# Rows of x stored in step order, the first expert's first 256 rows fetched and turned in the last two attention steps, and its first layer done in two column ranges

## The chip, the cores and the metric

The kernel runs on one core of one Trainium2 chip. The metric is the device time of one execution in microseconds (us). All tensors are float32 in memory. The engines are TensorE (PE, with its weight loads as PEld), VectorE (DVE), ScalarE (ACT), GpSimd (POOL) and SyncE (SP); SP, ACT and POOL also issue transfers (DMA), each through a queue of its own, in the order of the program.

## What is computed

Two blocks, one after the other. The first is an mLSTM cell over 4 batches, 8 heads, 768 positions and head width 40. Per head it carries a matrix state C, a normalizer n and a running maximum m, and its output is gated:

```python
m_new = np.maximum(f_gate[:, :, t] + m, i_gate[:, :, t])
f_stab = np.exp(f_gate[:, :, t] + m - m_new)
i_stab = np.exp(i_gate[:, :, t] - m_new)
C = f_stab * C + i_stab * outer(v_t, k_t);  n = f_stab * n + i_stab * k_t
y_t = sigmoid(o_gate_t) * (C @ q_t) / max(|n @ q_t|, 1.0)
```

(The broadcasts are shortened here.) Its output becomes x, 3072 rows of 320 numbers, one row per token, in the order batch, position. The second block is a mixture of 8 experts: a token goes to the expert that a hash of its id names, and the expert is two layers:

```python
expert_idx = token_ids * np.int64(2654435761) % np.int64(E)
for e in range(E):
    mask = expert_idx == e
    h = np.maximum(x[mask] @ w1[e], 0.0)     # w1: 320 x 1024
    out[mask] = h @ w2[e]                    # w2: 1024 x 320
```

## The kernel before

**Attention.** The cell is done in chunks of 128 positions. There are 24 steps, `for s in range(NT)` (L689); step s handles batch `s % 4` and chunk `s // 4` (`place`, L163). The order of instructions on every engine is written out by hand: each engine runs its instructions in program order and waits on semaphores. A step s does, in this order: transfers for later steps and the stores that are due (`waiting`, L711), on SP; `divided(s-1)` on DVE (L419 to L427: numerator by denominator, giving x of the step before); turns of keys and queries for s+2 (L304); pieces of the routing, spread over the steps by a table (`pieces`, L618); `scores(s+1)` (L350); `decays(s+1)` (L312: two exponentials on ACT, and `qs` on DVE, L332); up to two `gated` on POOL (L429: x times the output gate, L431); `state(s)` (L378); `weigh(s+1)` on DVE (L359, two instructions at L362); `attend(s)` on PE (L399, matmuls at L408 and L414). A gated tile is stored to the DRAM tensor `x_rows` two steps later (L736, `store` L433), at its token's place: row `b * S + c * P`.

**Routing.** Each token gets a slot: `route_counts` (L500) counts by one matmul, one scan along the 24 tiles and one addition the rank of each token among those of its expert; an expert has 416 slots, 384 in three tiles of 128 and 32 in a remainder that four experts share. `route_index` (L609, in step 21) makes from the slots two tables of row numbers: `g_idx`, from which rows are gathered, and `s_idx`, to which they are scattered. Tokens enter as numbers `tokv` (L445), which before follow batch and position, so that both tables hold the same numbers.

**Experts.** After the 24 steps come the last stores (L768), then the experts. `fetch(e)` (L863) issues on POOL three indirect gathers of 128 rows (L777) and, for the first expert of a group of four, a fourth for the remainder (`xr`). `turns(e)` (L872) turns each tile by three PE transposes (L797, L799, with a DVE copy of the last 64 columns between, L798) and a copy out of PSUM by DVE or ACT (L801, L803); the remainder's piece ends in a small POOL copy into the 32 last columns of `xT` (L883). `layer1` (L805) takes eight blocks of hidden features, two at a time: per pair four whole matmuls (L821) and two half-height ones (L814), each of 416 columns and each shown as two instructions in the profile, and two relus (DVE L828, ACT L830). `layer2` (L846) multiplies back (L850), and the rows are scattered (L784). Between the blocks of expert e, the tiles of expert e+1 are turned (`one`, L910), and for expert 0 the weights of experts 1 and 2 are asked for on ACT's queue.

At the border the order is: `fetch(0)`, `fetch(1)`, all four turns of expert 0, `fetch(2)`, `layer1` of expert 0 (L897 to L921). So POOL has seven gathers ahead of the copy L883. The PSUM banks of the experts are those of the attention steps, and become free with their last readers.

Of the kernel before, what the change touches and what calls it, by code (L numbers as in the profile page):

```python
# [8 lines left out]
F32 = mybir.dt.float32  # L9
BF16 = mybir.dt.bfloat16  # L10
I32 = mybir.dt.int32
I64 = mybir.dt.int64
AX = mybir.AxisListType.X
AF = mybir.ActivationFunctionType
ALU = mybir.AluOpType
PSUM = bass.MemoryType.PSUM

P = 128
# [4 lines left out]
def kernel(  # L23
# [24 lines left out]
    nc = tc.nc  # L48
    B, H, S, D = q.shape
    BH = B * H  # L50
    NB = S // P
    N = B * S
    Dm = H * D
    E, _, F = moe_w1.shape
    FB = F // P
    NT = N // P
# [1 line left out]
    DP = 64  # L58
    D1 = D + 1
    assert NB * P == S and FB * P == F and D <= DP and H % 2 == 0 and BH <= 32 and NB % 2 == 0  # L60
    assert E & (E - 1) == 0 and 2654435761 % E == 1

    dch = [(d0, min(P, Dm - d0)) for d0 in range(0, Dm, P)]
    DB = len(dch)

    NJ = 3
# [3 lines left out]
    CAP = NM + RM  # L70
    NR = E * NJ
    NX = -(-(N - CAP) // P)
    NC = NR + E // EG + NX
# [3 lines left out]
    wpools = [ctx.enter_context(tc.tile_pool(name="wpool", bufs=1))]  # L77
    w2pools = [ctx.enter_context(tc.tile_pool(name="w2pool", bufs=1))]

    x_d = nc.dram_tensor("x_rows", (N, Dm), F32, kind="Internal").ap()  # L80

    ident = consts.tile([P, P], F32, name="ident")
    g_idx = consts.tile([P, NC], I32, name="g_idx")
# [3 lines left out]
    def weights(src1, src2, wpool, w2pool, eng=None):  # L87

        eng = eng or nc.sync
        w1t = wpool.tile([P, 2, F], F32, name="w1t")  # L90
        w1c = wpool.tile([P, FB // 2, P], F32, name="w1c")
        w2t = w2pool.tile([P, FB, Dm], F32, name="w2t")
        eng.dma_start(w1t[:], src1[: 2 * P, :].rearrange("(a p) f -> p a f", p=P))
        last = src1[2 * P :, :].rearrange("d (a two f) -> two d a f", two=2, f=P)
        for i in range(2):
            eng.dma_start(w1c[i * P // 2 : (i + 1) * P // 2], last[i])
        eng.dma_start(w2t[:], src2.rearrange("(a p) d -> p a d", p=P))
        return w1t, w1c, w2t

    W = {}  # L100

# [30 lines left out]
    with tc.tile_pool(name="gates", bufs=1) as gp, \  # L132
# [30 lines left out]
        def place(s):  # L163
            return s % B, s // B
# [182 lines left out]
        def sigmoid(g):  # L347
            nc.scalar.activation(og[g][:], og[g][:], AF.Sigmoid)
# [82 lines left out]
            nc.gpsimd.tensor_tensor(x[:], x[:], og[s // NG][:, s % NG], op=ALU.mult)  # L431

        def store(s):  # L433
            b, c = place(s)
            r = b * S + c * P
            nc.sync.dma_start(x_d[r : r + P, :], st.pop(s)["x"].rearrange("p h d -> p (h d)"))

        iotas = {}
        for name, shape, pattern, base, mult in (
            ("experts", [P, E], [[1, E]], 0, 0),  # L440
            ("b2off", [P, E], [[-RM, E]], E * RM - RM, 0),
            ("thr", [P, NX], [[P, NX]], CAP, 0),
            ("kx", [1, NX], [[1, NX]], 0, 0),
            ("iota_f", [P, P], [[1, P]], 0, 0),
            ("tokv", [P, NT], [[P, NB], [S, B]], 1, 1),  # L445
        ):
            iotas[name] = (
                gp.tile(shape, I32, name=name + "_i"), gp.tile(shape, F32, name=name), pattern, base, mult,
            )
# [50 lines left out]
        def route_counts():  # L500
            cps = ps.tile([P, 2, E, NT], F32, name="cps", tag="tr", bufs=2)
            for i, t in enumerate((lt_m1, ones_sq)):
                nc.tensor.matmul(cps[:, i], lhsT=t[:], rhs=sel[:], start=True, stop=True)
            nc.vector.tensor_tensor_scan(
                pr.rearrange("p e t -> p (e t)"), keep_t.rearrange("p e t -> p (e t)"),
                cps[:, 1].rearrange("p e t -> p (e t)"), 0.0, op0=ALU.mult, op1=ALU.add,
            )
            nc.vector.tensor_tensor(rk[:], pr[:], cps[:, 0], op=ALU.add)

# [99 lines left out]
        def route_index():  # L609

            ta = gp.tile([P, NC], F32, name="ta")
            nc.vector.tensor_scalar(ta[:], tv[:], scalar1=-1.0, scalar2=0.0, op0=ALU.add, op1=ALU.max)
            nc.vector.tensor_copy(g_idx[:], ta[:])
            nc.vector.tensor_scalar(ta[:], tv[:], scalar1=0.0, scalar2=float(2 * N), op0=ALU.is_equal, op1=ALU.mult)
            nc.vector.scalar_tensor_tensor(ta[:], in0=tv[:], scalar=-1.0, in1=ta[:], op0=ALU.add, op1=ALU.add)
            nc.vector.tensor_copy(s_idx[:], ta[:])

        pieces = {  # L618
# [12 lines left out]
        o_at = {}  # L631
        for i, j in enumerate((2, 2, 3, 3, 4, 4, 5, 5, 6, 7, 8, 8, 9, 10, 10, 11, 12, 13, 13, 14, 15, 15, 16, 16)):
            o_at.setdefault(j, []).append(i)

        def unread(n):
            t = ps.tile([P, P], F32, name="un", tag="xh", bufs=2)
# [52 lines left out]
        for s in range(NT):  # L689
# [43 lines left out]
            for i in range(2):  # L733
                if ndone < s and ndone // NG <= nsig and s - 1 not in sig_at:
                    gated(ndone)
                    waiting.setdefault(min(s + 2, NT), []).append(ndone)  # L736
                    ndone += 1
            state(s)
            if s + 1 < NT:
# [6 lines left out]
            if s in sig_at:  # L746
                nsig = sig_at[s]
                sigmoid(nsig)
            attend(s)
            if s == 2:  # L750
                g1.weights(kwT1)
            if s == 3:
# [20 lines left out]
    xp = ctx.enter_context(tc.tile_pool(name="xp", bufs=2))  # L773
    mps = ctx.enter_context(tc.tile_pool(name="mps", bufs=2, space=PSUM))

    def gather(xg, idx):
        nc.gpsimd.indirect_dma_start(  # L777
            out=xg, out_offset=None, in_=x_d[:, :], in_offset=bass.IndirectOffsetOnAxis(ap=idx, axis=0),
        )

    def scatter(zp, idx, apart):
        zo = xp.tile([P, Dm], F32, name="zo", bufs=4)
        nc.scalar.copy(zo[:], zp[:])  # L783
# [18 lines left out]
        else:  # L802
            nc.vector.tensor_copy(dst, tp[:])  # L803

    def layer1(w, xT, h, cols, between=lambda fp: None):  # L805

        w1t, w1c, _ = w
        for fp in range(FB // 2):
            hp = [mps.tile([P, CAP], F32, name="mh", bufs=4) for _ in range(2)]

            def halves(first):
                for i in range(2):
                    r = slice(i * P // 2, (i + 1) * P // 2)
                    nc.tensor.matmul(  # L814
                        hp[i][:, :cols], lhsT=w1c[r, fp, :], rhs=xT[r, 2, :cols], start=first, stop=not first,
                    )

            def whole(i, first):
                fb = 2 * fp + i
                for db in range(2):  # L820
                    nc.tensor.matmul(  # L821
                        hp[i][:, :cols], lhsT=w1t[:, db, fb * P : (fb + 1) * P], rhs=xT[:, db, :cols],
                        start=(first and db == 0), stop=(not first and db == 1),
                    )

            def out(i):
                if i == 0:
                    nc.vector.tensor_relu(h[:, 2 * fp, :cols], hp[i][:, :cols])  # L828
                else:
                    nc.scalar.activation(h[:, 2 * fp + 1, :cols], hp[i][:, :cols], AF.Relu)  # L830

            if fp % 2 == 0:
                for i in range(2):
                    whole(i, True)
                between(fp)
                halves(False)
                for i in range(2):
                    out(i)
            else:
                halves(True)  # L840
                for i in range(2):
                    whole(i, False)
                    out(i)
                between(fp)
# [15 lines left out]
    with tc.manual_schedule():  # L860
        xgs, xTs, remT, hrem = {}, {}, {}, {}

        def fetch(e):  # L863
            if e % EG == 0:
                xgs[-1 - e // EG] = xp.tile([P, DB * P], F32, name="xr")
            xgs[e] = xp.tile([P, NJ, DB * P], F32, name="xg", bufs=3)
            for j in range(NJ):
                gather(xgs[e][:, j, :Dm], cols_of(g_idx, e * NJ)(j))
            if e % EG == 0:
                gather(xgs[-1 - e // EG][:, :Dm], cols_of(g_idx, NR + e // EG)(0))  # L870

        def turns(e):  # L872
            xT = xTs[e] = xp.tile([P, DB, CAP], F32, name="xT")

            def tile_of(j):
                turn(xgs[e][:, j, :], xT[:, :, j * P : (j + 1) * P], j % 2 == 1)

            def remainder():
                i = e % EG
                if i == 0:  # L880
                    remT[e // EG] = xp.tile([P, DB, P], F32, name="remT")
                    turn(xgs[-1 - e // EG], remT[e // EG][:], True)
                nc.gpsimd.tensor_copy(xT[:, :, NM:], remT[e // EG][:, :, i * RM : (i + 1) * RM])  # L883

            return [lambda j=j: tile_of(j) for j in range(NJ)] + [remainder]
# [10 lines left out]

        fetch(0)  # L897
        fetch(1)
        for piece in turns(0):
            piece()  # L900
        for e in range(E):
            g, i = e // EG, e % EG
            if e + 2 < E:
                fetch(e + 2)
            h = xp.tile([P, FB, CAP], F32, name="h")
            if i == 0:
                hrem[g] = xp.tile([P, EG, FB, RM], F32, name="hrem")
            ahead = turns(e + 1) if e + 1 < E else []
# [9 lines left out]
                if j == 0 and i == EG - 1:  # L918
                    rest(g)

            layer1(W[e], xTs[e], h, CAP, one)  # L921
            nc.gpsimd.tensor_copy(hrem[g][:, i], h[:, :, NM:])  # L922
            layer2(W[e], h, NJ, cols_of(s_idx, e * NJ), True, after)
            if e + 3 < E:
# [3 lines left out]
    with tc.If(nx > 0):  # L928
        with tc.For_i(0, nx, 1) as k:
# [10 lines left out]
            h = xp.tile([P, FB, CAP], F32, name="h")  # L940
            gather(xr[:, :Dm], gs[:, 0:1])
            turn(xr, xT[:, :, :P], False)
            layer1(w, xT, h, P)
            layer2(w, h, 1, lambda j: gs[:, 1:2], False)


# [28 lines left out]
```

## Time and profile before

| | us |
|---|---|
| median of 3 runs | 400.91 (400.55 to 402.49) |
| the profiled execution | 402.59 |
| its span, first to last instruction | 400.8 |
| PE busy | 370.8 (93%) |
| POOL busy | 144.4 (36%) |
| DVE busy | 137.7 (34%) |
| ACT busy | 111.9 (28%) |
| clock granted to PE, mean over the span | 0.964 |

The page divides the span into 40 slices of 10.02 us; a digit is the busy share in tenths. The timeline lists instructions by start, length, engine, line, and output and inputs; "idle before" names how long the engine stood still and what ended it. The chain of waits follows the last instruction back to whatever released each step. Matmul ends are modelled, and neighbours overlap in the listing, so I take distances from start to start where a stream is dense.

### The profile page before, as it was taken

The numbers are of one execution on the slowest core, as the hardware profiler recorded it, in microseconds if no ns is written. First come the engines' busy times: TensorE is split into PE (matmuls) and PEld (weight loads), VectorE is DVE, ScalarE is ACT, GpSimd is POOL, SyncE is SP. The second block draws the span as 40 slices with busy tenths as digits, with TensorE's granted clock in tenths as the row PEclk, the third lists the DMA queues.
The fourth block names the chain that finished last, engine by engine and source line by source line (L and its number), as shares of the span: only waits on it lengthen the run. The fifth ranks groups of instructions, "written<-read, shape, count | busy, mean of one in ns | idle before, by whom it ended". The sixth has DMA issues, their size and how long they took to land.

```text
span 400.8 us, 7874 instructions
## 1 busy us (share of the span) xinstructions
PE 370.8 (93%) x3163; PEld 253.5 (63%) x3163; DVE 137.7 (34%) x345; ACT 111.9 (28%) x227; POOL 144.4 (36%) x247
## 2 busy tenths in 40 slices
PE   8699879999999728999999999999999999999992
PEld 8487668788888614565575575555575575574561
DVE  8657657797878711201202101101201101101100
ACT  5386475566485200110101101101110101101100
POOL 8342428897987254014025013025024011010020
PEclk9899998999999956999999999999999999999997
DMA  6688998989899338892082182252092000000000
GB/s 133 122 157 147 172 172 158 200 174 196 172 224 264 117 94 276 272 338 80 7 281 87 34 271 65 82 179 87 18 278 84 2 33 15 2 33 16 0 20 32
DMA packets 124220, 51.02 MB, mean 127 GB/s; under 512 B 104338, under 2 KB 120174, under 8 KB 124182
## 3 DMA queue, kind: packets, MB, share of 16 engines
q1 hardware_dynamic: 116614, 36.73, 39.4%
q0 software_dynamic: 2496, 8.20, 6.5%
q10 hardware_dynamic: 5072, 5.57, 4.6%
q8 instruction: 26, 0.43, 0.4%
q14 instruction: 12, 0.10, 0.1%
HBM read 42.10 MB, written 8.71 MB: 127 GB/s over the span
## 4 chain that ended last, share of the span: by engine, by line
PE 71%; issue 8%; POOL 8%; DMA 5%; DVE 3%; ACT 2%; SPq 2%; POOLq 0%; DVEq 0%; ACTq 0%
PE mh L821 23%; PE zp L850 23%; PE mh L814 6%; PE tr L309 4%; PE sp L356 4%; POOL x L431 3%; PE xh L414 2%; PE ab L320 2%; PE tp L797 1%; PE xh L408 1%; PE xh L387 1%; PE zp L891 1%; POOL C L397 1%; DMA x_rows<-x 1%; DMA xr<-x_rows,g_idx 1%
## 5 line engine op out<-in xcount | busy, mean ns | idle before, releaser
L850 PE MATMUL zp<-w2t,h 128*128 128x320 f32 x384 | 105.2, 433 | 0.0
L821 PE MATMUL mh<-xT,w1t 128*128 128x416 f32 x256 | 98.4, 529 | 0.9 <-issue 0.9
L850 PEld LDWEIGHTS zp<-w2t,h 128*128 128x128 f32 x384 | 72.7, 190 | 32.1 <-issue 3.3
L821 PEld LDWEIGHTS mh<-xT,w1t 128*128 128x128 f32 x256 | 47.7, 194 | 44.0 <-issue 42.9
L784 POOL DMA_INDIRECT out_dram<-zo,s_idx x26 | 25.7, 987 | 92.5 <-ACT zo L783 92.5
L803 DVE COPY xT<-tp 128x384 f32<-128x384 f32 x16 | 8.9, 558 | 142.5 <-PE tp L799 103.2
L830 ACT ACTIVATE h<-mh 128x416 f32<-128x416 f32 x32 | 16.6, 517 | 109.6 <-PE mh L814 59.8
L783 ACT COPY zo<-zp 128x320 f32<-128x320 f32 x26 | 11.1, 426 | 101.1 <-PE zp L850 92.9
L828 DVE TENSOR_SCALAR h<-mh 128x416 f32<-128x416 f32 x32 | 18.9, 592 | 53.4 <-PE mh L821 26.9
L414 PE MATMUL xh<-v,w 128*64 128x41 f32 x768 | 34.8, 222 | 0.3 <-DVE w L362 0.3
L362 DVE TENSOR_TENSOR w<-sp,w 128x512 f32<-128x512 f32 x48 | 30.8, 682 | 12.2 <-ACT w L324 12.2
L922 POOL COPY hrem<-h 128x256 f32<-128x256 f32 x8 | 3.2, 400 | 83.7 <-ACT h L830 83.7
L324 ACT ACTIVATE w<-ab 128x512 f32<-128x512 f32 x48 | 26.0, 594 | 18.9 <-PE ab L320 18.9
L414 PEld LDWEIGHTS xh<-v,w 128*64 128x64 f32 x768 | 30.7, 138 | 0.4 <-DVE w L362 0.4
L356 PE MATMUL sp<-qT,kT 64*128 64x128 f32 x384 | 30.0, 294 | 0.1
L356 PEld LDWEIGHTS sp<-qT,kT 64*128 64x128 f32 x384 | 25.0, 195 | 4.4 <-issue 2.8
L408 PE MATMUL xh<-C,qs 128*64 128x82 f32 x320 | 27.4, 250 | 0.0
L777 POOL DMA_INDIRECT xg<-x_rows,g_idx x24 | 23.5, 978 | 9.7 <-issue 9.7
L814 PE MATMUL mh<-xT,w1c 64*128 64x416 f32 x128 | 26.7, 535 | 0.0
L397 POOL TENSOR_TENSOR C<-C,add 64x164 f32<-64x164 f32 x32 | 17.7, 553 | 20.8 <-ACT add L391 19.6
L431 POOL TENSOR_TENSOR x<-x,og 128x320 f32<-128x320 f32 x24 | 20.5, 871 | 9.4 <-DVE x L427 9.4
L309 PE MATMUL tr<-ident,q 128*128 128x128 f32 x96 | 15.3, 283 | 4.6 <-ACT dec L334 2.5
(177 smaller groups left out, 390.6 us busy)
## 6 DMA issues: line engine op xcount, KB each, us to landing
w2t<-in_moe_w_dram SPq DMA_DIRECT2D x5, 1280.0 KB
w1t<-in_moe_w_dram SPq DMA_DIRECT2D x5, 1024.0 KB
k<-in_k_dram SPq DMA_DIRECT2D x24, 160.0 KB
v<-in_v_dram SPq DMA_DIRECT2D x24, 160.0 KB
og<-in_o_gate_dram SPq DMA_DIRECT2D x24, 160.0 KB
x_rows<-x SPq DMA_DIRECT2D x24, 160.0 KB
q<-in_q_dram SPq DMA_DIRECT2D x23, 160.0 KB
w2t<-in_moe_w_dram ACTq DMA_DIRECT2D x2, 1280.0 KB
```

The costliest lines, as they stand in the source:

```text
L309: nc.tensor.transpose(tp[:, j, :], d[what][:, 2 * j : 2 * j + 2, :].rearrange("p h d -> p (h d)"), ident[:])
L324: nc.scalar.activation(w[:, hf], ab[:], AF.Exp)
L356: nc.tensor.matmul(sp[hf][:, j, :], lhsT=d["kT"][r, j, :], rhs=d["qT"][r, j, :], start=True, stop=True)
L362: nc.vector.tensor_tensor(d["w"][:, hf], d["sp"][hf][:], d["w"][:, hf], op=ALU.mult)
L408: nc.tensor.matmul(xh[t, 2 * j : 2 * j + 2, :], lhsT=d["qs"][:, j, t], rhs=Cs[b][c % 2][:, j].rearrange("p h d -> p (h d)"), start=True, s ...
L414: nc.tensor.matmul(hs[t, 2 * j + hf, :], lhsT=d["w"][:, hf, j, t], rhs=d["v"][:, 2 * j + hf, :], start=(c == 0), stop=True, skip_group_che ...
L431: nc.gpsimd.tensor_tensor(x[:], x[:], og[s // NG][:, s % NG], op=ALU.mult)
L777: nc.gpsimd.indirect_dma_start(out=xg, out_offset=None, in_=x_d[:, :], in_offset=bass.IndirectOffsetOnAxis(ap=idx, axis=0),)
L784: ins = nc.gpsimd.indirect_dma_start(out=out[:, :], out_offset=bass.IndirectOffsetOnAxis(ap=idx, axis=0), in_=zo[:], in_offset=None, bound ...
L814: nc.tensor.matmul(hp[i][:, :cols], lhsT=w1c[r, fp, :], rhs=xT[r, 2, :cols], start=first, stop=not first,)
L821: nc.tensor.matmul(hp[i][:, :cols], lhsT=w1t[:, db, fb * P : (fb + 1) * P], rhs=xT[:, db, :cols], start=(first and db == 0), stop=(not fir ...
L850: nc.tensor.matmul(zp[:], lhsT=h[:, fb, j * P : (j + 1) * P], rhs=w[2][:, fb, :], start=(fb == 0), stop=(fb == FB - 1),)
```

## The change

There are four parts.

1. Row s * 128 + p of `x_rows` now holds position p of step s. `tokv` counts in that order, and `route_index` works the token's number out of the row number for `s_idx` alone.
2. The first 256 slots of expert 0 take only tokens of the first 20 steps (`TE = 20`): if it had fewer than 256 there, its later tokens are moved up to rank 256 by two instructions in `route_counts`.
3. Tiles from 19 on are stored one step after their gating and not two; at the end of step 21 POOL gathers expert 0's first two tiles from the first 20 * 128 rows; at the end of step 22 DVE copies their last columns and PE and ACT turn the first, and the second is turned in step 23 ahead of `attend(23)`. They have buffers of their own (`xg0`, `xT0`, `h0`).
4. `fetch(0)` asks for the third tile and the remainder alone. `layer1` takes a column range; expert 0 does columns 0 to 256, then turns the third tile and the remainder, then columns 256 to 416. These turns now come behind `fetch(2)` in the program.

```diff
+    TE = N // P - B
+    xg0 = early.tile([P, NJ, DB * P], F32, name="xg0")
+    xT0 = early.tile([P, DB, CAP], F32, name="xT0")
+    h0 = early.tile([P, FB, CAP], F32, name="h0")
...
         def store(s):
-            b, c = place(s)
-            r = b * S + c * P
-            nc.sync.dma_start(x_d[r : r + P, :], ...)
+            nc.sync.dma_start(x_d[s * P : (s + 1) * P, :], ...)
...
-            ("tokv", [P, NT], [[P, NB], [S, B]], 1, 1),
+            ("tokv", [P, NT], [[P, NT]], 1, 1),
...
+            dn = gp.tile([P, 1], F32, name="dn")
+            nc.vector.tensor_scalar(
+                dn[:], pr[:, 0, TE - 1 : TE], scalar1=-1.0, scalar2=float(2 * P), op0=ALU.mult, op1=ALU.add,
+            )
+            nc.vector.scalar_tensor_tensor(
+                pr[:, 0, TE:], in0=dn[:].to_broadcast([P, NT - TE]), scalar=0.0, in1=pr[:, 0, TE:], op0=ALU.max, op1=ALU.add,
+            )
             nc.vector.tensor_tensor(rk[:], pr[:], cps[:, 0], op=ALU.add)
...
             nc.vector.tensor_copy(g_idx[:], ta[:])
+            ti = gp.tile([P, 2, NC], I32, name="ti")
+            tf = gp.tile([P, 2, NC], F32, name="tf")
+            nc.vector.tensor_scalar(
+                ti[:, 0], g_idx[:], scalar1=7, scalar2=B - 1, op0=ALU.arith_shift_right, op1=ALU.bitwise_and,
+            )
+            nc.vector.tensor_scalar(ti[:, 1], g_idx[:], scalar1=9, scalar2=None, op0=ALU.arith_shift_right)
+            nc.vector.tensor_copy(tf[:], ti[:])
...
+            nc.vector.scalar_tensor_tensor(ta[:], in0=tf[:, 0], scalar=float(S - P), in1=ta[:], op0=ALU.mult, op1=ALU.add)
+            nc.vector.scalar_tensor_tensor(ta[:], in0=tf[:, 1], scalar=float(P - B * P), in1=ta[:], op0=ALU.mult, op1=ALU.add)
             nc.vector.tensor_copy(s_idx[:], ta[:])
...
+        def early_turn(j):
+            tp = ps.tile([P, DB, P], F32, name="tpx", tag="tr", bufs=2)
+            for db in range(DB):
+                nc.tensor.transpose(tp[:, db, :], xg0[:, j, db * P : (db + 1) * P], ident[:])
+            nc.scalar.copy(xT0[:, :, j * P : (j + 1) * P], tp[:])
...
-                    waiting.setdefault(min(s + 2, NT), []).append(ndone)
+                    waiting.setdefault(min(s + 1 + (s < NT - B - 1), NT), []).append(ndone)
...
+            if s == NT - 1:
+                early_turn(1)
             attend(s)
+            if s == NT - 3:
+                for j in range(2):
+                    gather(xg0[:, j, :Dm], g_idx[:, j : j + 1], TE * P)
+            if s == NT - 2:
+                for j in range(2):
+                    nc.vector.tensor_copy(xg0[:, j, Dm:], xg0[:, j, 2 * P : Dm])
+                early_turn(0)
...
-    def layer1(w, xT, h, cols, between=lambda fp: None):
+    def layer1(w, xT, h, c0, c1, between=lambda fp: None):
...
-            for j in range(NJ):
+            for j in range(NJ) if e else (2,):
                 gather(xgs[e][:, j, :Dm], cols_of(g_idx, e * NJ)(j))
...
         fetch(0)
         fetch(1)
-        for piece in turns(0):
-            piece()
         for e in range(E):
...
-            layer1(W[e], xTs[e], h, CAP, one)
+            if e == 0:
+                layer1(W[0], xT0, h0, 0, 2 * P)
+                for piece in turns(0)[2:]:
+                    piece()
+            layer1(W[e], xTs[e], h, 2 * P if e == 0 else 0, CAP, one)
```

## The prediction

> **What bounds the kernel now.** I read the page's forty slices first, for where PE is not busy. Only one hole is large, at slices 14 and 15, and the granted clock falls there too:
>
> ```profile
> PE   8699879999999728999999999999999999999992
> PEclk9899998999999956999999999999999999999997
> ```
>
> That is 140 to 160 us, the border between attention and experts. Then the chain of waits over 137 to 153 us says what fills the hole:
>
> ```profile
> 139.16 0.86 POOL x L431
> 140.02 0.02 issue
> 140.03 1.77 DMA x_rows<-x
> ...
> 141.96 0.86 issue
> 142.83 1.21 POOL xg L777
> ...
> 146.86 3.76 DMA xr<-x_rows,g_idx
> 150.62 0.14 issue
> 150.76 0.66 PE tp L797 x2
> 151.42 0.21 PE tp L799
> 151.63 0.90 issue
> 152.53 1.06 PE mh L821
> ```
>
> The last attend ends at 137.89 (PE timeline). Its rows are divided, gated (0.86), stored (1.77), and after 1.02 more the first gather starts; four gathers follow each other, and the fourth, for the remainder, lands at 150.62. So the first layer starts at 152.53, 14.64 us after the last attend. Its clock then is a second loss. The windows view:
>
> ```profile
> 138.00:139.50 1.50, 0.00 (x0) 1.00 0.18 64
> 139.50:140.00 0.50, 0.00 (x0) 0.95 0.39 136
> 140.00:146.00 6.00, 0.00 (x0) 0.50 0.18 55
> ...
> 156.50:157.00 0.50, 0.50 (x2) 0.50 1.49 381
> 157.00:157.50 0.50, 0.50 (x3) 0.98 0.91 199
> ```
>
> The third number from the right is the clock: it halves about 2.1 us after PE's last matmul and comes back at about 157.0, 4.5 us after dense work began. Expert 0's first layer takes 18.23 us (152.53 to 170.76), expert 1's 15.74 (183.68 to 199.42) with the same matmuls and three turns: the cold start costs 2.5. From 170.76 on PE has no hole, so what reaches that moment earlier ends earlier.
>
> The DVE timeline bounds the steps ahead of the border:
>
> ```profile
> 128.99 0.86 DVE L613 CAST g_idx<-ta 128x47 int32<-128x47 f32 x1
> 129.88 0.19 DVE L614 TENSOR_SCALAR ta<-tv 128x47 f32<-128x47 f32 x1
> 130.10 0.21 DVE L615 SCALAR_TENSOR_TENSOR ta<-tv,ta 128x47 f32<-128x47 f32 x1
> 130.34 0.19 DVE L616 CAST s_idx<-ta 128x47 int32<-128x47 f32 x1
> 130.46 0.69 DVE L332 TENSOR_TENSOR qs<-qT,xb 128x512 f32<-128x512 f32 x1
> 131.06 1.28 DVE L362 TENSOR_TENSOR w<-sp,w 128x512 f32<-128x512 f32 x2
> ```
>
> No row here shows an idle time before it: from 125.54 to 137.4 DVE has no gap, so an instruction added to it in step 21 is paid.
>
> **Part 1, row numbers.** The stores move as many bytes as before. `route_index` gets five DVE instructions behind `g_idx`; its neighbours go start to start in 0.22, so 5 x 0.22 = 1.1 us. `qs` of step 22 stands behind them (130.46, while its PSUM operand was ready at about 130.4), then `weigh(22)`, which frees the score banks for PE, then `qs` and `weigh` of step 23. I see no cover and count +1.1 on all of it; were the slack larger than the listing shows, it would be 0.
>
> **Part 2, ranks.** Two small DVE instructions stand ahead of `rk` (47.3, step 5), some 0.35 to 0.4 by the small rows of that stage (0.13 to 0.17 each, start to start 0.2). DVE idles 1.59 soon after (before `qs` at 50.30), but PE waits: `cps` shares its two PSUM buffers with the turns, and the turn at 47.77 follows the end of `rk` after 0.71 idle. The chain runs from that turn over SP to a transfer. Between 0 and 0.4; I take 0.4, since the turn's start is the chain's own.
>
> **Part 3, early gathers and turns.** In the built order the first early gather waits for the stores of tiles 0 to 19 and for `g_idx`. `gated(19)` ends at 127.19; its store, now in step 21, is issued behind it at about 127.3. The one clean row for a store is 1.77, so 129.1; with the DMA 0.87 busy there I allow 130.5 (another transfer of that stage took 2.94). `g_idx` is there at 129.85, as before. With 1.02 of start-up the gathers start near 131.0 and 132.5 (1.51 apart before). Landing took 3.3 from the first start before (142.83 to 146.12) and 3.76 at most: 134.3 to 136.3. Behind them on POOL stand `gated(21)` to `gated(23)`; the first of these needs x at 133.4 + 1.1, when POOL is done with the gathers at about 133.5, so nothing waits. DVE reaches the copies behind `weigh(23)`, at 136.33 + 1.1 = 137.4, so the rows are in time by 1 to 3 us.
>
> The two copies (0.2 by L798, with start to start 0.23) add 0.45 to DVE, ending 137.85; `divided(22)` stands behind them and runs to 138.9. On PE six turns, 0.33 per tile (L797 and L799 when warm: 0.22 + 0.11), stand ahead of `attend(23)`; the last cannot start before the second copy, so they end near 138.05. An attend without a wait takes 1.65 (134.22 to 135.86), so the last one ends at 139.7, not 137.89: **+1.8**. `divided(23)` took 1.13 and ends at 140.9. The last gating, store and full-range gather move by the same 1.8: that gather starts at 144.63.
>
> **Part 4, the first layer.** Its first matmul waits, in the built order, for `divided(23)` (PSUM reuse): range A starts at 140.9. PE idles 1.2 there, less than the 2.1 after which the clock fell before, so A is warm. Warm, eight whole instructions of 416 columns took 2.79, 0.84 ns a column; 320-column ones 12.92 / 48 = 0.269, again 0.84. So 256 columns take 0.215, and 32 of them 6.9. The half-height ones run in pairs, eight in 1.60, 0.2 each, of which 0.175 is columns: 0.13 each at 256, 16 make 2.1. With 0.4 for refills (2.99 less 2.79, twice) A is 9.4 and ends at **150.3**. Before, this time was idle.
>
> Meanwhile POOL issues eight gathers from 144.63: 1.51, then six times 1.255, then 0.95 make 154.6. The third tile lands at about 148, the remainder by 149.9; both are turned by 151.6, remT copied by 152.1. But the POOL copy L883, 0.27, stands behind `fetch(2)` now, and range B's first matmul waits for it: **154.95**. Before, it stood ahead of `fetch(2)` and waited only for remT.
>
> B has 160 columns: 32 x 0.134 = 4.3, 16 x 0.092 = 1.5, refills 0.4, three turns of expert 1 1.0: 7.2 warm. The weights are loaded a second time, and a load must now fit into 0.134. The loads list as 0.19, but turns with a 128x128 load each go at 0.118 to 0.127 apiece, so I add nothing; loads at 0.19 would add 1.8. PE idles from 151.6 to 154.95, 3.4 us, above the 2.1 of before, so I take B to start cold: between 0 and 2.5, I take 2.3. B ends at 154.95 + 9.5 = **164.45**.
>
> The page "TensorE: Matmul & The Clock Gate", section "HAM oscillation — how this bites in real kernels", warns of PE idle gaps above about 3.4 us; its window would make this gap a matter of phase, B ending at 162.2 or 164.5. The trace's fall after 2.1 us speaks for the cold end.
>
> **The sum.** 170.76 - 164.45 = 6.3 gained, less 0.4 of part 2: 5.9. Against the profiled execution 402.6 - 5.9 = 396.7. That execution lies 1.7 above the median of 400.9; the forecast in terms of the median is **395.0**. The weights of experts 1 and 2 are asked for at about the same time (ACT's issue was at 151.67 behind the remT copy and is now at 152.1), and expert 1 starts 6 us sooner, near 177; in the windows view the DMA's dense stretch ended at 162, so they are there.
>
> **The rivals.**
>
> *B stays warm, or DVE's extra is hidden.* For it: the gap of 3.4 has turns ahead of it, and PE's wait on DVE in step 22 is short. Against it: the fall after 2.1. Gains 2.3 and up to 1.5 more: 391.2 to 392.7, say 392.5.
>
> *The early rows land late.* The gathers now run beside a busy DVE and a DMA at 0.75 to 0.87; all gathers in the trace of before ran beside an idle or lightly used DVE. One row shows the two engines in each other's way: the cast at 128.99 took 0.86 while POOL gated for 0.86, its sister at 130.34 0.19. Each us by which the second tile lands after 137.6 delays DVE, PE and the last store by one: 2 us late give 397.
>
> The page "SBUF — State Buffer", section "SBUF: two separate sides", speaks against the change here: descriptors that GpSimd writes for a gather wait while DVE holds the port they share, 620 ns becoming 3100. By that price, an estimate, both early gathers land 2.5 to 5 later, up to 3.7 past need, and the sum would be near 398.7. No run here shows it yet.
>
> *Slower than before.* The same mechanism carried further, at one place: POOL held in the early gathers. Since the copies stand in DVE's order ahead of `divided(22)`, all of the last two steps hangs on them. It turns the gain of 5.9 into a loss when the second tile lands after 137.6 + 5.9 = 143.5, and into one beyond 0.5% after 145.5; a landing at 147 gives 404.4. Nothing in the profile takes 12 us from a gather's start to its landing (3.76 is the longest I found at the border).
>
> *It does nothing for the time.* If B waits so long for POOL's copy that A's gain is eaten: the copy would have to come 6 us later, at 161. POOL's gathers are regular to 0.05, so 3 in 100.
>
> **How the numbers follow.** Forecast 395.0, its own range 393.5 to 396.5: 0.55. Warm or hidden, 392.5: 0.18. Late rows, 397: 0.15. Near 401: 0.05. Slower, 404.4: 0.07. The range leaves out 0.2 at most: from 391.5 to 399.0, which takes in a warm B, both ends of parts 1 and 2, the loads at 0.19 and 4 us of lateness. A measurement of this kernel tells 0.5% from no change, about 2 us: faster means below 398.9, which the first three cases give, 0.88; within 0.05; slower 0.07.
>
> **What would show it.** Right: matmuls of 256 columns start near 141 at clock 1.0 and end near 150; the first 160-column one starts directly after POOL's remT copy near 155, behind eight gathers; clock 0.5 somewhere in 153 to 158; layer 2 of expert 0 starts near 164. Wrong: PE waiting for the early gathers ahead of `attend(23)`; A starting later than 142 or running cold; 160-column instructions taking 0.19 when warm; new holes after 165, where the order of gathers or weights would have hurt.

## The result and the profile after

The changed kernel takes **406.19 us** (median of 4 runs, 405.22 to 406.89), the kernel before 400.73 in the same set (399.78 to 402.49). The ratio is 1.0129 [1.0086, 1.0173]: slower, by about 5.2 us, where 395.0 was forecast. The profiled execution took 406.89, with a span of 405.0 (402.59 and 400.8 before).

In the changed kernel's page, the forty slices (now 10.1 us each) show that the border did improve: where slices 13 to 15 read 7, 2 and 8 before, 13 to 16 now read 8, 7, 8 and 7, and the clock falls to 6 in one slice there and not to 5 and 6 in two. But slices 1, 3 and 6 read 5, 8 and 6 where they read 6, 9 and 9, the clock in slice 6 is a 6, and the DMA row is a 9 in thirteen of its first fourteen slices:

```profile
PE   8598896999998878799999999999999999999992
PEclk9789996999999999699999999999999999999998
DMA  9799999999999943897183192053182000000000
...
q1 hardware_dynamic: 116614, 36.73, 46.0%
```

The last line is the queue that carries the ordinary loads and stores: packets, MB, and the time that its packets took as a share of 16 engines' span. The same two lines of the page of before:

```profile
DMA  6688998989899338892082182252092000000000
...
q1 hardware_dynamic: 116614, 36.73, 39.4%
```

Packets and bytes are equal to the last digit. The time they took is not: 39.4% of 400.8 is 157.9 us per DMA engine, 46.0% of 405.0 is 186.3. The change moves no byte more and yet costs 28 us of each DMA engine.

**Where the time went.** I compared the starts of equal instructions, the score matmuls (`sp`) on the PE timeline. Those of step 0 start at 8.88 before and 8.98 after, those of step 1, which are done in step 0, at 17.55 and 19.27, those of step 10 at 67.33 and 72.88, of step 19 at 113.91 and 119.42, of step 22 at 128.48 and 136.22. So 1.7 us are lost within step 0, 5.5 up to the score matmuls of step 10, none in the next nine steps, and 7.7 up to those of step 22. The first instruction that the diff touches makes `tokv`, at 28.59, when 2.0 us are lost already. On the PE timeline (start, length, instruction, what ended the idle time ahead of it in square brackets) one of the turns that wait for keys in step 0 reads, before:

```profile
16.05 0.63 PE L309 MATMUL tr<-ident,k 128*128 128x128 f32 x4 [2.12 <-DMA k<-in_k_dram]
```

and after, where the line numbers of the attention are 12 higher:

```profile
17.14 1.09 PE L321 MATMUL tr<-ident,k 128*128 128x128 f32 x4 [3.21 <-DMA k<-in_k_dram]
```

The same load lands 1.1 later. The windows view gives the stages ahead of the border: length, busy time of PE, PEld, DVE, ACT and POOL, and as the last three numbers the clock, the mean busy share of the DMA engines and the GB/s they moved. Before:

```profile
2.00:10.00 8.00, 8.00 (x58) 7.71 (x57) 7.67 (x18) 5.22 (x8) 7.70 (x32) 1.00 0.80 162
20.00:60.00 40.00, 35.52 (x666) 30.00 (x662) 25.81 (x69) 26.10 (x55) 14.05 (x35) 0.99 0.90 162
```

After:

```profile
2.00:10.00 8.00, 7.52 (x57) 7.14 (x56) 7.46 (x18) 5.22 (x8) 7.70 (x31) 1.00 1.22 152
20.00:60.00 40.00, 37.32 (x680) 31.77 (x676) 26.20 (x70) 21.48 (x50) 13.74 (x35) 0.96 1.05 149
```

The engines are busier (a share above 1 means that the packets of one engine overlap in the records) and move less. What is different about these transfers is where they land. In the addresses of the built programs, the new buffers `xg0`, `xT0` and `h0` (4608 + 4992 + 13312 = 22,912 B per partition) lie ahead of the attention's tiles, and `dn`, `ti` and `tf` among them; all that follows moves up. A tile of keys or queries has a place of 256 B per head, of which one transferred piece fills 160 B. Its start moves from 96 to 480 modulo 512. So before, a piece covered bytes 96 to 256 of a 256-byte line; after, it covers 224 to 384 and **crosses into the next line**. That concerns 48 loads of 1024 pieces each, 49,152 of the 116,614 packets.

**The border after.** The chain of waits of the changed kernel, start and length of each step:

```profile
141.47 1.20 POOL xg L108
142.67 0.30 issue
142.97 2.91 DMA xg<-x_rows,g_idx
146.01 0.52 PE tpx L664 x3
...
149.42 0.87 POOL x L443
150.31 1.75 DMA x_rows<-x
...
152.83 0.99 POOL xg L108
...
161.62 0.95 POOL xg L108
162.57 1.45 issue
164.01 0.27 POOL xT L919
164.33 2.50 PE mh L857 x8
```

The early rows land at 145.88 and the second tile's turn follows; the last gated rows are stored by 152.06; eight gathers run from 152.83 to 162.57; the POOL copy L919 (the former L883) comes after 1.45 more, and range B starts. Range A lies in this stretch, on the PE timeline from 149.48:

```profile
149.48 1.97 PE L857 MATMUL mh<-xT,w1t 128*128 128x256 f32 x8 [1.32 <-DVE x L439]
...
164.33 2.50 PE L857 MATMUL mh<-xT,w1t 128*128 128x160 f32 x8 [2.61 <-POOL xT L919]
```

Layer 2 of expert 0 starts at 174.97. Counted from the score matmul of step 22, that is 38.75, against 170.76 - 128.48 = 42.28 before: the border gives 3.5, and the stage ahead of it takes 7.7.

### The profile page after: what moved, and what is told of

Its sections match the earlier page's. It is cut to its first block, busy times and chain, and to the rows that moved or that the text cites. A ratio compares the mean times of both kernels' runs of the same rounds, so it can differ in the third digit from the quotient of the medians.

```text
span 405.0 us, 7980 instructions
## 1 busy us (share of the span) xinstructions
PE 372.7 (92%) x3211; PEld 260.8 (64%) x3211; DVE 138.6 (34%) x355; ACT 113.0 (28%) x232; POOL 144.0 (36%) x247
## 3 DMA queue, kind: packets, MB, share of 16 engines
q1 hardware_dynamic: 116614, 36.73, 46.0%
## 4 chain that ended last, share of the span: by engine, by line
PE 66%; POOL 9%; issue 6%; DMA 6%; DVE 6%; ACT 5%; POOLq 0%; SPq 0%; DVEq 0%; ACTq 0%
PE zp L886 22%; PE mh L857 21%; PE mh L850 6%; PE tr L321 3%; PE sp L368 3%; DMA R<-gate_pieces 2%; PE xh L426 2%; POOL xg L108 2%; ACT og L360 2%; PE ab L332 2%; POOL x L443 1%; PE tp L833 1%; DVE w L374 1%; PE xh L420 1%; PE zp L927 1%
## 5 line engine op out<-in xcount | busy, mean ns | idle before, releaser
L857 PE MATMUL mh<-xT,w1t 128*128 128x416 f32 (+2 forms) x288 | 98.6, 488 | 3.9 <-POOL xT L919 2.6
L857 PEld LDWEIGHTS mh<-xT,w1t 128*128 128x128 f32 x288 | 52.6, 195 | 42.6 <-issue 38.0
L866 ACT ACTIVATE h<-mh 128x416 f32<-128x416 f32 (+2 forms) x36 | 17.2, 478 | 113.3 <-PE mh L850 60.5
L864 DVE TENSOR_SCALAR h<-mh 128x416 f32<-128x416 f32 (+2 forms) x36 | 19.6, 543 | 60.1 <-PE mh L850 29.0
L850 PE MATMUL mh<-xT,w1c 64*128 64x416 f32 (+2 forms) x144 | 28.1, 509 | 0.4 <-DVE h L864 0.4
```

What stands on the lines that cost most here:

```text
L850: nc.tensor.matmul(hp[i][:, : c1 - c0], lhsT=w1c[r, fp, :], rhs=xT[r, 2, c0:c1], start=first, stop=not first,)
L857: nc.tensor.matmul(hp[i][:, : c1 - c0], lhsT=w1t[:, db, fb * P : (fb + 1) * P], rhs=xT[:, db, c0:c1], start=(first and db == 0), stop=(not ...
```

## The experiments

Theory L (layout): the loss is the transfers' slower time at their new addresses; no instruction of the change costs it. Theory S (schedule): the added instructions, stores and gathers cost it. The kernels of one set share the runs of the kernel before, whose median is given with each set.

### First set (before: 400.56): the layout alone, and the change without it

**The change at the old addresses.** A pad behind `h0`, another among the routing's tiles and a shared place for `ti` put keys and queries back at 96 modulo 512; every instruction of the change stays.

```diff
+    pad = early.tile([P, 32], F32, name="pad")
+    gpad = gp.tile([P, 24], F32, name="gpad")
-            ti = gp.tile([P, 2, NC], I32, name="ti")
+            ti = iotas["iota_f"][0][:, : 2 * NC].rearrange("p (a c) -> p a c", a=2)
```

> The changed kernel with 128 bytes of padding behind the new buffers and 96 in the routing pool (one new integer tile placed in a dead one), so that every tile a transfer fills starts at the address modulo 512 that it had before the change. Theory L (layout): the 22,912 bytes of new buffers moved the key and query tiles from 96 to 480 modulo 512, so that each 160-byte piece of a row crosses a 256-byte line, and the transfers of the attention stage take longer; with the old addresses modulo 512 the time falls to 396, within 1.5, and the hardware queue's share of the DMA engines to 39 or 40%. Theory S (schedule): the stores one step earlier, the rank instructions and the early gathers delay the steps; nothing of that is taken away, so 406 and 46%.

Measured: 396.58, ratio 0.9905 [0.9876, 0.9934]. Its queue, with a span of 393.7:

```profile
q1 hardware_dynamic: 116614, 36.73, 40.1%
```

That is 157.9 us per engine, as before the change. This is what theory L expected.

**The kernel before at the new addresses.** An unused buffer of the same size, and a second one of 800 B among the routing's tiles; no instruction differs.

```diff
+    early = ctx.enter_context(tc.tile_pool(name="early", bufs=1))
+    pad = early.tile([P, 5728], F32, name="pad")
+    gpad = gp.tile([P, 200], F32, name="gpad")
```

> The kernel before, with an unused buffer of 22,912 bytes where the change puts its own and 800 in the routing pool, so that its tiles lie where those of the changed kernel lie; no instruction differs. Theory L: the attention stage is as slow as in the changed kernel, 7.7 us by the score matmuls of step 22, so 408 within 2, queue share 45% or more. Theory S: 400.7, share 39.4%.

Measured: 411.09, ratio 1.0263 [1.0231, 1.0294]: **10.5 us for buffers that nothing reads or writes.** The queue, with a span of 409.5, takes 186.7 us per engine:

```profile
q1 hardware_dynamic: 116614, 36.73, 45.6%
```

**The change, keys and queries at 0 modulo 512.** All else stays where the change put it, within 32 B.

```diff
+    pad = early.tile([P, 8], F32, name="pad")
```

> The changed kernel with 32 bytes of padding: key and query tiles start at 0 modulo 256, so a 160-byte piece starts on a 256-byte line and crosses none. Theory L, if what counts is crossing a line: as a_old_layout, 396 within 1.5. If a start off the line costs as well: faster than a_old_layout, 393 to 395. Theory S: 406.

Measured: 396.12, 0.9891 [0.9862, 0.9919]; 39.3% of 396.4 is 155.8 us per engine. 32 bytes bring back the whole loss.

**The kernel before, keys and queries at 256 modulo 512.**

```diff
+    early = ctx.enter_context(tc.tile_pool(name="early", bufs=1))
+    pad = early.tile([P, 40], F32, name="pad")
```

> The kernel before with 160 bytes of padding: key and query tiles start at 0 modulo 256 instead of 96; no instruction differs. If only crossing counts: 400.7 within 1. If a start off the line counts: 398 to 400. Theory S: 400.7.

Measured: 400.52, 0.9994 [0.9972, 1.0016]; the queue takes 39.0% of 399.9, 156.0. A start at the head of a line is no better than one at 96, as long as the piece ends within the line. So the start alone is not what costs.

### Second set (before: 400.64): which tiles, and is it the crossing

**Only keys and queries moved**, to 480. `kpad` lies ahead of the keys; `qpad`, behind the queries, puts what follows back (modulo 512).

```diff
+        kpad = gp.tile([P, 96], F32, name="kpad")
+        qpad = gp.tile([P, 32], F32, name="qpad")
```

> The kernel before with padding ahead of the key tiles (384 bytes) and behind the query tiles (128), so that only those twelve tiles move, from 96 to 480 modulo 512. If the pieces of k and q that cross a 256-byte line carry the whole loss of the changed kernel's layout: 408 to 411, as b_new_layout's 411.1. If other tiles carry it: 400.6.

Measured: 408.85, 1.0218 [1.0182, 1.0253]; 45.3% of 406.7 is 184.2 us per engine. Its window of 20 to 60 us shows the change's state without the change:

```profile
20.00:60.00 40.00, 37.16 (x680) 31.54 (x676) 25.85 (x68) 21.34 (x49) 13.87 (x35) 0.97 1.06 149
```

**Keys and queries at 128 modulo 256**, a start that is a multiple of 64 and 128, whose piece ends at 288 and so crosses (pads of 8 and 120 floats in place of 96 and 32).

> The same with 32 bytes ahead and 480 behind: keys and queries start at 128 modulo 256, a rounder address than before's 96, but each 160-byte piece now reaches 32 bytes over a 256-byte line. If crossing the line is what costs: 408 to 411, as b_kq_480. If what counts is a start at a multiple of 64 or 128: 400.6 or faster.

Measured: 408.78, 1.0238 [1.0189, 1.0288]; 45.2% of 407.0, 184.0. It costs the same as 480: **the crossing decides**, not the alignment of the start. The size of the line is less certain: with places 256 B apart, half of the pieces that cross a 256-byte line here cross a 512-byte line too, and none of those within a line does. No version parts the two.

**All but keys and queries moved** to the change's addresses modulo 512.

```diff
+    pad = early.tile([P, 5728], F32, name="pad")
+        kpad = gp.tile([P, 32], F32, name="kpad")
+        qpad = gp.tile([P, 96], F32, name="qpad")
+        gpad = gp.tile([P, 72], F32, name="gpad")
```

> The kernel before with everything where the changed kernel has it, modulo 512, except keys and queries, which stay at 96. If k and q carry the whole loss: 400.6 within 1. If values, output gates or gate rows carry a part: up to 411, the part that b_kq_480 does not show.

Measured: 399.56, 0.9976 [0.9955, 0.9996]; 157.6 us per engine. The other tiles' places cost nothing; nor do 22,912 B of buffer as such. But 8.2 us for keys and queries and nothing for the rest leave 2.3 of the 10.5 without a place; the two intervals, 1.0182 to 1.0253 and 1.0231 to 1.0294, overlap.

**The change with `fetch(2)` behind the last turns**, on top of the 32-byte pad. In the changed kernel POOL's copy L919 stands behind the three gathers of `fetch(2)`, and range B's first matmul waits for it.

```diff
+            if e == 0:
+                layer1(W[0], xT0, h0, 0, 2 * P)
                 for piece in turns(0)[2:]:
                     piece()
+                fetch(2)
...
-            if e + 2 < E:
+            if 0 < e < E - 2:
                 fetch(e + 2)
```

> The changed kernel with aligned keys and queries (a_kq_aligned, 396.1), and the three gathers of expert 2 issued behind the remainder's turn and not ahead of it, so that POOL's copy of the remainder stands behind five gathers and not eight. Theory P (POOL's queue holds range B): B can start when the turned remainder is out of PSUM, 1 to 3.5 us earlier, 393 to 395. Theory T (the turns of the third tile and the remainder hold it anyway): 396.1, no change.

Measured: **391.68**, 0.9789 [0.976, 0.9819]; it beats both kernels. Its ratio is 1.0 points below that of the kernel with the pad alone (about 4.1 us), more than the 1 to 3.5 that were expected. The POOL timeline shows the copy between the last needed gather and the first of `fetch(2)`:

```profile
146.84 0.95 POOL L109 DMA_INDIRECT xg<-x_rows,g_idx  x1 [0.30 <-issue]
150.47 0.26 POOL L920 COPY xT<-remT 128x96 f32<-128x96 f32 x1 [2.69 <-ACT remT L838]
150.89 0.98 POOL L109 DMA_INDIRECT xg<-x_rows,g_idx  x1 [0.16 <-issue]
```

PE starts range B directly behind it and reaches layer 2 at 158.79 to 158.95:

```profile
150.79 1.35 PE L858 MATMUL mh<-xT,w1t 128*128 128x160 f32 x8 [0.94 <-POOL xT L920]
...
158.79 13.08 PE L887 MATMUL zp<-w2t,h 128*128 128x320 f32 x48
```

B takes 8.16 and runs warm in this execution, so the version gains twice. Counted from the score matmul of step 22, against the kernel with the pad alone, B starts 2.5 earlier (25.27 against 27.75; 0.7 of it was there when range A started) and takes 1.6 less (8.16 against 9.74, which began as the clock fell). The expectation had the first alone.

### Third set (before: 400.21): the five DVE instructions, and other tensors

**The scatter's indices after the last step.** On top of the version above, what makes `s_idx` stands behind `divided(NT - 1)`, so that the five added instructions leave step 21.

```diff
+        def route_scatter():
+            ta = gp.tile([P, NC], F32, name="ta2")
...
         divided(NT - 1)
+        route_scatter()
```

> a_fetch2_late (391.7) with the work on the scatter table taken out of step 21 and put behind the last division, where DVE idles: five added and three old instructions, 1.6 us in all. The prediction's term: the five instructions cost 1.1 since DVE has no gap in steps 21 to 23; then the distance from the score matmuls of step 22 to the second layer, 33.4 in a_fetch2_late, falls by 1.1 to 1.9 and the time to 390.0 to 390.7. If they were covered: no change, 391.7 and 33.4.

Measured: 391.47, 0.978 [0.9748, 0.9813], no difference from 0.9789 [0.976, 0.9819] that can be told. The term itself is there, in the profiled executions: from the score matmul of step 22 to that of step 23 the version above takes 4.31, this one 3.40, before 3.41. But the turn of the second tile then waits longer for the early rows (0.98), and in the profiled execution range B began at clock 0.5, and layer 2 started 34.5 behind the score matmul of step 22, against 33.4. So here the 0.9 was won in step 22 and did not reach the end. The mean clocks of the single runs say that this is not so in every execution: the two runs of this version at 0.992 took 390.43 and 389.85, as expected or less, its four at 0.984 to 0.987 took 391.45 to 393.69; of the version above, four runs at 0.990 to 0.992 took 390.87 to 391.89 and two at 0.982 and 0.987 took 393.14 and 393.0. At a like clock the late indices look about 1 us faster; too few runs show it to settle it.

**Values and output gates, all pieces within a line.** Their heads were packed (164 and 160 B apart), so that by their addresses 29 of 48 (values) and 32 of 64 (gates) pieces crossed.

```diff
-        vs = [gp.tile([P, H, D1], F32, name=f"v{i}") ...]
+        vs = [gp.tile([P, H, DP], F32, name=f"v{i}")[:, :, :D1] ...]
-            og[...] = ld.tile([P, NG, H, D], F32, ...)
+            og[...] = ld.tile([P, NG, H, DP], F32, ...)[:, :, :, :D]
+        gpad = gp.tile([P, 24], F32, name="gpad")
```

> The kernel before with the heads of values and output gates laid 256 bytes apart in SBUF (before: 164 and 160), so that none of their 160-byte pieces crosses a 256-byte line; before, 29 of 48 in the value tiles and 32 of 64 in the gate tiles did. If each crossing piece costs the same wherever it is, 49,152 crossing pieces of k and q having added 26 us per DMA engine, 27,136 fewer take 14 off: queue share 36%. Time, by the same proportion as the 8.2 us of b_kq_480: up to 4.5 less, 396 to 400. If only k and q are sensitive: 39.4% and 400.6.

Measured: 399.59, 0.9988 [0.9971, 1.0004]; 39.2% of 396.5 is 155.4 us per engine, 2.5 less than before and not 14 less. The expectation missed: either a crossing in a packed row costs next to nothing, or the gaps cost about what the missing crossings save. No run parts these two.

### Fourth set (before: 400.56): is it a property of keys and queries

**The same two tensors 128 B further on**, so that all their pieces cross (a pad of 32 floats ahead of the values, 96 behind, 56 in place of 24 ahead of the gates).

> b_v_og_inside (399.6, queue share 39.2%) with values and output gates moved 128 bytes on, so that every one of their pieces, still 256 bytes apart, crosses a 256-byte line. If a crossing piece costs whenever its neighbours do not lie against it (heads 256 apart), whichever tensor it belongs to: 26 us more per DMA engine, share 45% or more, 407 to 411, and then the earlier lack of gain is because pieces that lie against each other (160 or 164 apart) cross at no cost. If values and gates are insensitive for another reason: 399.6 and 39%.

Measured: 404.27, 1.0084 [1.0056, 1.0113]; 41.9% of 402.2 is 168.5, which is 13.1 above the version within the line. So it is no property of keys and queries: pieces with gaps between them cost more when they cross. But the size is half of the 26 that was expected.

**The keys alone at 480**, queries within the line (`kpad` ahead of the keys, `qpad` between them and the queries).

```diff
+        kpad = gp.tile([P, 96], F32, name="kpad")
+        qpad = gp.tile([P, 32], F32, name="qpad")
```

> b_kq_480 with the keys alone moved to 480 modulo 512. If each crossing piece costs the same: half of the 26 us per DMA engine, share 42.5%, and 402 to 407. If the loss comes from q or from both meeting: 400.6 or 408.9.

Measured: 403.14, 1.0044 [1.0017, 1.0071]; 41.3% of 401.7 is 165.9, 8.0 above before. Keys and queries together cost 26.3 (184.2 less 157.9), so the keys alone cost less than a third, not half: the price is not so much per crossing piece.

## Why the prediction was wrong

**The step that failed is the ground of the sum.** It read "170.76 - 164.45 = 6.3 gained, less 0.4 of part 2: 5.9", and every time in it ("`gated(19)` ends at 127.19", "at 136.33 + 1.1 = 137.4") was taken from the trace of before, as if the first 20 steps could not move but by part 2. The new buffers `xg0`, `xT0` and `h0` had no term at all. Of the transfers it asked only for bytes ("The stores move as many bytes as before"), and not where the loads' pieces land. The missing term is +7.7 us at the score matmul of step 22; the layout alone costs 10.5 in the kernel before, and keys and queries alone 8.2. With that term taken out by padding, the change measures 396.1 to 396.6, in the forecast's own range of 393.5 to 396.5 or 0.1 above. The slower rival (POOL held in the early gathers) did not happen, and the one with late rows only by half a microsecond; the forecast's 0.07 for a slower kernel was for another cause.

Point by point, at the border, counted from the score matmul of step 22, which takes the shift out:

- **Whole border.** Forecast 6.3 earlier; the changed kernel gives 3.5, the padded versions 5.1 (37.2, old addresses) and 4.8 (37.5, 32-byte pad).
- **Five DVE instructions, +1.1.** Right: 3.41 became 4.31, +0.9, and taking them away gave 3.40.
- **Part 2, 0.4.** Nothing: two score matmuls of that stage lie 5.85 apart before (42.48 to 48.33) and 5.84 in the version with the 32-byte pad (42.53 to 48.37).
- **Last attend, +1.8.** It ends 9.41 after the score matmul of step 22 before and 11.94 after: +2.5. The early rows landed at 145.88 and DVE stood still for 0.62 ahead of the second copy; that is the late-rows rival, at half a microsecond. The first early gather started 5.25 after that score matmul, and 4.1 to 4.3 in the padded versions, where POOL waited for a store; the forecast had 2.5. In the padded versions the rows were in time and the last attend still ended 2.5 (old addresses) and 2.9 (32-byte pad) later than before. There a `gated` of POOL stood directly behind the second early gather, and a small DVE instruction of step 22 (L550) that began during this gather took 1.08 and 1.39 and ended 0.03 and 0.04 after that `gated`; in the changed kernel, where it fell between the two gathers, it took 0.17. The forecast had seen DVE and POOL in each other's way once, at the cast at 128.99, and gave it no term here. The two early gathers themselves took 1.20 and 0.96 beside a busy DVE, the same as the first gathers of before beside an idle one (1.21 and 0.96). The price that the prediction took from the Trainium skill's page "SBUF — State Buffer", section "SBUF: two separate sides", is not seen in these rows. That section ties it to certain DVE instructions, a float32 copy within SBUF among them; no such copy ran while these two gathers did, so they do not test it.
- **Range A, 9.4 and warm.** Right: 149.48 to 158.99, 9.5.
- **Eight gathers, 9.97.** Right: 9.74.
- **The remT copy ready ahead of L883.** Wrong: L919 waited 1.45 more, since DVE's copy of the third tile started 1.1 after PE's turn (1.8 and 1.1 in the padded versions), and ACT's copy of the remainder 1.75 after its turn (0.4 and 1.1). In the two versions whose `fetch(2)` stands behind these turns, DVE's copy started 0.4 to 0.5 and ACT's 0.1 after. What held them was not tried by itself.
- **Range B cold, 9.5.** In kind right: 10.6, and 9.7 in the padded versions, with the clock of the changed kernel down from 162.8 to 169.6. PE's gaps there were 1.65 and 2.61, each shorter than the 3.4 that the prediction cites. Warm it takes 8.16 (`fetch(2)` late), not 7.2: the whole matmuls 0.136 as forecast (0.134), the half-height ones 0.135 each and not 0.092, and 0.41 of a wait for DVE's relu.

The order of parts was seen rightly, that POOL's copy stands behind `fetch(2)`. The prediction left it at that; moving it was worth 4.1.

## What to carry to other kernels

A buffer that is added is an edit of every address behind it: compare the built addresses of the tiles that many small transfers write, before and after, and ask whether a piece crosses a 256-byte line that it did not cross before. When a change slows a stage that it does not touch, compare the DMA queue's time at equal packets and bytes, and build the kernel before with an unused buffer of that size; this settles layout against instructions in one run. A sum over one border holds only if the time at which that border starts is a term of the sum.

## What the runs showed of the hardware

- **Crossing a 256-byte line.** Pieces of 160 B, 256 B apart, take 156.0 (start at 0) and 157.9 us (start at 96) of queue time per engine within the line, and 184.2 and 184.0 across it (224, 128). 26 us over 49,152 / 16 = 3072 pieces an engine is some 8.6 ns a piece, an estimate. What the DMA engine does in it is not in the trace, and whether it is the 256-byte line or, for half of the pieces, the 512-byte line is not parted.
- The Trainium skill's page "DMA: Bandwidth & Descriptors", section "How a descriptor splits into AXI transactions", says that a read begins at the 256-byte boundary below its start and that the bytes in between cost beats. By its rule, as an estimate, a piece takes 5 beats from 0, 8 from 96 and 12 in two transactions from 224. That fits the runs in that the crossing costs; that 0 and 96 are equal (400.52 against 400.56) does not follow from its beats, and the page speaks of reads, while here it was the place written that moved.
- **Not additive, and no price seen when packed.** Keys alone +8.0, keys and queries +26.3, values and gates with gaps +13.1, and packed rows, half of whose pieces cross, within 2.5 of none crossing. Why is open.
- **26 to 30.5 us of queue time became 8 to 10.5 us of kernel time**, about a third; 8.0 us for the keys alone became 2.6. In the changed kernel the delay grew where a transfer was waited for: in step 0 (keys), by 0.5 ahead of the score matmuls of step 6, by 2.6 ahead of those of step 9, and again from step 19 on; between the score matmuls at 67 and 114 it stayed at 5.5. Ahead of those of step 9, ACT's sigmoid of the output gate waits for a transfer 4.7 us, 2.5 before.
- **The clock can fall after the work has come back.** In the version with the 32-byte pad PE had a gap up to 156.59; the windows view of PE (length, busy time, clock, DMA share, GB/s) shows full clock in the gap's last stretch and the fall in dense work:

```profile
156.00:157.00 1.00, 0.41 (x3) 1.00 0.94 188
157.00:158.00 1.00, 1.00 (x6) 0.63 0.70 152
```

A shorter gap, to 150.79, left the clock full in the profile of the version with `fetch(2)` late, while in the version with late scatter indices the clock fell at 149.9 in the like gap. The length of the gap alone did not decide.
